# Offering the denominators' products some time behind the modelled landing of p, and starting both chains of them one block of f sooner

## The chip, the cores and the metric

The kernel runs on one core of a Trainium2 chip. Its engines are TensorE (PE in the profile; PEld is its weight load), VectorE (DVE), ScalarE (ACT), GpSimd (POOL) and SyncE (SP). Here POOL and SP mostly issue DMA transfers, each from a queue of its own: q0 is POOL's and q1 is SP's. The metric is the device time of one execution in microseconds, as the median of several runs.

## The reference, cut to what matters

The input x has 2048 tokens of 640 columns. The output is a mix of two branches, weighted by a gate per token:

```
g   = sigmoid(sum(x * gate_w))
# branch a: linear attention, 32 heads of 20
q, k, v = x @ wqkv, split by heads
phi(t)  = (t + 1 if t > 0 else exp(t)) + 1e-6
kv  = sum over tokens of phi(k)^T v ;  z = sum over tokens of phi(k)
num = phi(q) @ kv ;  den = phi(q) . z + 1e-6
a   = (num / den) @ wo
# branch b: gated linear unit, 1536 wide
b   = (sigmoid(x @ w_gate) * (x @ w_up)) @ w_down
out = g * a + (1 - g) * b
```

The change concerns `den`: the sum, over the 20 elements of a head, of phi(q) times z.

## The kernel before, in words

All products are done in three TensorE passes on operands split in a high and a low part (`mm3`, lines 404 to 406). The splitting is work for ScalarE (line 417) and VectorE (line 421), so that both engines are busy with preparing operands and with taking results out of PSUM while TensorE multiplies. Many products use a two by two scheme with sums of operands (steps s1 to s7 of `Block`), which saves products and costs sums.

The tokens are in four groups `g` of 512. First come the keys, kv and z, and M = kv @ wo, which is stored in `m_dram`. Then the groups 2 and 3 (`pr` = 1) and afterwards the groups 0 and 1 (`pr` = 0) go through two phases. `q_phase` makes p = phi(q) and stores it in `p_dram`. `f_phase` runs over 12 blocks `f` of 128 hidden columns of branch b: the steps 3, 4, 5 of block f, step 1 of block f + 1, step 6 of f, step 2 of f + 1 and step 7 of f. From f = 3 on, an odd block also holds the down products of the pair of blocks before it (`down_pair`), so that odd blocks are about twice as long as even ones. At the end M, scaled p and the sums of branch b are put together.

In the phase of `pr` = 0 the weights come back from scratch memory in their split form: `load_form` loads the tiles `wg`, `wu` and `ws` of block f + 2 after steps 2, 6 and 7 of f, and `load_wf` loads, after an odd block, the three pieces of `wf` for the next down products. All these loads are issued by SP. Meanwhile rows of M are loaded by SP into `mr`, split into `mt`, and stored by POOL in `mp_dram` (`queue_m`).

The denominators are made by `queue_dens` (line 1399), in one chain for the groups 2 and 3 and another for 0 and 1. With the heads interleaved over the partitions, phi(q) . z is a sum of five terms, one per slice u of 128 columns: p of that slice times a column of z, added to `fac[:, g]`. So a chain has these links, in this order:

- load p of u = 0 and 1 for both groups into `pden` (POOL's queue);
- for each u and each group, one product on VectorE (line 1412 for u = 0, line 1414 for the others; the profile shows them as L432 and L425), behind which the load of u + 2 is issued;
- behind the last product of a group, the store of `den_dram`;
- `turn_in`: four loads per group that fold the four partial sums of a head side by side (POOL), and a load of the gates `gs` (SP);
- `factor`: the sums, the reciprocal, the product with the gate (VectorE), and the store of `fac_dram` (POOL);
- `turn_out`: four loads per group that spread the factors over `fac` (SP).

The order of instructions is fixed while the program is written, by a planner, the class `Order`. It keeps a modelled clock for TensorE, ScalarE and VectorE, and a model of the two DMA queues (`Ring` and `Rings`, lines 303 to 361) which gives each transfer a modelled landing. Side work waits in lists. `fill` (line 115) is called after each unit of TensorE's work and takes side work as long as it fits: its modelled end must lie no more than a set slack behind TensorE's clock, and the function `ready` that came with it must give a time that has been reached (`_fits`, line 107). The lists are tried in this order: urgent, the streams with due times, items, lazy, chain, spare. Of `chain` only the first entry is looked at, so an entry that isn't ready holds up the rest of the chain, and the `spare` list gets its turn. The denominators are in `chain`; the splits of M are in `spare`. On the chip each engine carries out its instructions in the order so fixed, and real waits are made by semaphores.

For a product `one(g, u)` the time `ready` is the modelled landing of its p, `st["at", g, u]()`. The table `dens` (line 2011) says at the start of which block of f the two chains are put in the list, for the phase of `pr` = 0.

Of the kernel before, what the change touches and what calls it, by code (L numbers as in the profile page):

```python
# [19 lines left out]
TG = 512  # L20
# [9 lines left out]
class Order:  # L30
# [121 lines left out]
    def _stream(self):  # L152
        best = None
        for name, q in self.streams.items():
            if q and (q[0][4] is None or max(self.pe, self.act if q[0][0] else self.vec) >= q[0][4]()):
# [4 lines left out]
                if best is None or d < best[0]:  # L160
                    best = (d, name)
        if best and (best[0] <= self.pe + EARLY or self._fits(self.streams[best[1]][0])):
            return best[1]
# [136 lines left out]
            self.seeded[out.tensor.name] = at  # L300

EARLY = 2.0
class Rings:

    def __init__(self):
# [62 lines left out]
def v_cost(w):  # L368
    return 0.07 + w / 960

@with_exitstack
def gated_mix_kernel(ctx: ExitStack, tc: tile.TileContext, xt, xn, wk, wv, wo, wst_q, wst_f, out_t):
# [6 lines left out]
    order = Order()  # L379
# [39 lines left out]
    def vec2(out, a, b, op, after=""):  # L419
        order.on_vec(width(out), after, 1.0, out, a, b)  # L420
        nc.vector.tensor_tensor(out, a, b, op=op)  # L421

    def vec3(out, a, scalar, b, op0, op1, after=""):
        order.on_vec(width(out), after, 1.0, out, a, b)
        nc.vector.scalar_tensor_tensor(out, a, scalar, b, op0=op0, op1=op1)  # L425

    def vec1(out, a, s0, s1=None, op0=OP.mult, op1=None, after=""):
        order.on_vec(width(out), after, 1.0, out, a)
        if op1 is None:
            nc.vector.tensor_scalar(out, a, s0, None, op0=op0)  # L430
        else:
            nc.vector.tensor_scalar(out, a, s0, s1, op0=op0, op1=op1)  # L432
# [10 lines left out]
    def add(out, a, b, after=""):  # L443
        vec2(out, a, b, OP.add, after)
# [574 lines left out]
    g = GTBatch(0, [0])  # L1019
# [8 lines left out]
    for c in range(1, 4):  # L1028
        ck = chunks[c]
        if c == 1:  # L1030
# [14 lines left out]
            g = GTBatch(c, batches[c])  # L1045
# [97 lines left out]
        if c > 1:  # L1143
            g = GTBatch(c, batches[c])
# [50 lines left out]
    def tt(name, dt=F32, shape=(P, TG)):  # L1195
        return pw.tile(list(shape), dt, name=name, tag="t", bufs=4)
# [202 lines left out]
    def queue_dens(*gs2):  # L1399

        st = {}

        def load(g, u):
            if u < KC:
                st[g, u] = tt("pden")
                gp.dma_start(st[g, u], p_dram[:, u, g])
                st["at", g, u] = lambda: order.when(st[g, u])

        def one(g, u):
            td = fac[:, g]  # L1410
            if u == 0:
                vec1(td, st[g, u], zcol[:, 0:1], zeps[:, 0:1], OP.mult, OP.add)
            else:
                vec3(td, st[g, u], zcol[:, u:u + 1], td, OP.mult, OP.add)
            load(g, u + 2)
            if u == KC - 1:
                gp.dma_start(den_dram[:, g], td)
                st["at", g, u + 1] = lambda: order.when(den_dram[:, g])

        def turn_in(g):  # L1420
            for j in range(4):
                js = slice(j * H, (j + 1) * H)
                gp.dma_start(fac[js, g].rearrange("h (d c) -> h d c", c=P),
                                  den_dram[:, g, j * P:(j + 1) * P].rearrange("(d h) c -> h d c", h=H))
            st[g, "gs"] = tt("gs")[:, :P]
            sp.dma_start(st[g, "gs"], gate_rep[4 * g:4 * g + 4].rearrange("i h c -> (i h) c"))
            st["at", g, KC + 1] = lambda: max(order.when(fac[:, g]), order.when(st[g, "gs"]))

        def factor(g):
            td = fac[:, g]  # L1430
            q = td[:, :P]
            add(td[:, :2 * P], td[:, :2 * P], td[:, 2 * P:])
            add(q, q, td[:, P:2 * P])
            order.on_vec(5 * P, "")
            nc.vector.reciprocal(q, q)
            vec2(q, q, st[g, "gs"], OP.mult)
            gp.dma_start(fac_dram[:, g], q)
            st["at", g, KC + 2] = lambda: order.when(fac_dram[:, g])

        def turn_out(g):  # L1440
            for d in range(4):
                sp.dma_start(fac[d * H:(d + 1) * H, g].rearrange("h (j c) -> h j c", c=P),
                                  fac_dram[:, g].rearrange("(j h) c -> h j c", h=H))
        order.add(0, 0, lambda: [load(g, u) for u in range(2) for g in gs2], chain=True)
        for u in range(KC):
            for g in gs2:
                order.add(0, v_cost(TG), lambda g=g, u=u: one(g, u), None, lambda g=g, u=u: st["at", g, u](), chain=True)
        for n, (v, fn) in enumerate(((0, turn_in), (2.0, factor), (0, turn_out))):
            for g in gs2:
                order.add(0, v, lambda g=g, fn=fn: fn(g), ("fac", g) if n == 2 else None,  # L1450
                          lambda g=g, n=n: st["at", g, KC + n](), chain=True)
# [556 lines left out]
            phi_q(2 * pr + 1, 0, B.c12, "v")  # L2008
        order.slack(False)

    dens = ({3: (2, 3), 7: (0, 1)}, {})

    def f_steps(f):
        down = f % 2 and f > 1
# [8 lines left out]
    def f_phase(pr, q, hooks={}):  # L2023
# [7 lines left out]
        for f, s in [(0, 1), (0, 2)] + [e for f in range(FC) for e in f_steps(f)]:  # L2031
            order.plan[pr, f, s] = at
            at += mm * n_mm[s]
        order.plan[pr, FC + 1, "d0"] = at - EARLY

# [53 lines left out]
        for f in range(FC):  # L2089
# [3 lines left out]
            if f in dens[pr]:  # L2093
                queue_dens(*dens[pr][f])
# [514 lines left out]
```

## Time and profile before

| what | value |
| --- | --- |
| median of 3 runs | 736.67 us |
| lowest and highest run | 735.58 and 737.15 us |
| span of the profiled execution | 733.0 us |
| TensorE busy | 726.8 us, 99% |
| VectorE busy | 561.7 us, 77% |
| ScalarE busy | 355.1 us, 48% |
| loads of pden by POOL | 20, first and last issued at 448.6 and 567.4 us |
| products of the denominators | 20, first and last begun at 481.2 and 575.0 us |
| granted clock of TensorE | 1.000 |

The span reaches from the first to the last instruction in the profile. The profile does not list a device time of the profiled execution itself, so the span is compared with the times of the runs, which are 2.6 to 4.2 us above it. Of a busy engine the sum of busy time says little here; what counts is at which place TensorE pauses, and for whom.

In the profiled execution the phase of `pr` = 0 has its block f = 2 from about 468 to 481 us, f = 3 to 505, f = 4 to 518, f = 5 to 542, f = 6 to 555, f = 7 to 580 and f = 8 to 593.

In the views, a row of the order of time has the start, the duration, the engine, the line and the operation, "out<-in", and in brackets how long the engine stood idle before it and what ended that. A row of a table by stage has the stage, its length, then the busy time and number of instructions of PE, PEld, DVE, ACT and POOL, the granted clock, the share of the DMA engines and their GB/s. A row of waits has the waiting instruction, whom it waited for, the total, the number of times and the longest. A row of DMA issues has the transfer, the queue, the number, the size, and the median time from issue to landing.

### The profile page before, as it was taken

How to read it: one execution, taken by the hardware profiler on the slowest of the kernel's cores; microseconds unless marked ns; L12 is line 12 of the kernel's file. 1: busy time of each engine (PE TensorE's matmuls, PEld its weight loads, DVE VectorE, ACT ScalarE, POOL GpSimd, SP SyncE). 2: the span in 40 equal slices, each digit the busy share in tenths (PEclk: the TensorE clock that was granted, in tenths of full speed). 3: DMA queues.
4: the chain of work that ended last, by engine and by line, in shares of the span. 5: the costliest groups of instructions: out<-in, count | busy, mean ns of one | idle time of the engine just before them, and what ended most of it. 6: DMA issues, size and time to landing. Idle time of an engine off the chain costs nothing.

```text
span 733.0 us, 10118 instructions
## 1 busy us (share of the span) xinstructions
PE 726.8 (99%) x3575; PEld 622.9 (85%) x3575; DVE 561.7 (77%) x987; ACT 355.1 (48%) x661; POOL 113.9 (16%) x197
## 2 busy tenths in 40 slices
PE   9999999999999999999999999999999999999998
PEld 8999999988788888888888888888887888888886
DVE  4978777987677889898989942566766775689976
ACT  5765648357556653535355363354332232332541
POOL 0211111113211211111211212023011231000000
PEclk9999999999999999999999999999999999999999
DMA  8564748697877866557687568878978596759212
GB/s 268 128 192 112 187 114 249 151 352 265 300 270 264 328 241 236 184 218 253 259 326 267 214 230 292 317 231 281 356 266 317 179 322 197 276 209 372 80 67 102
DMA packets 68873, 173.54 MB, mean 237 GB/s; under 512 B 11690, under 2 KB 31418, under 8 KB 65238
## 3 DMA queue, kind: packets, MB, share of 16 engines
q1 hardware_dynamic: 50342, 103.70, 42.7%
q0 software_dynamic: 18336, 69.03, 26.9%
q8 instruction: 28, 0.46, 0.2%
q14 instruction: 23, 0.19, 0.1%
q10 hardware_dynamic: 144, 0.16, 0.1%
HBM read 103.96 MB, written 63.92 MB: 229 GB/s over the span
## 4 chain that ended last, share of the span: by engine, by line
PE 86%; DMA 6%; issue 3%; DVE 2%; ACT 1%; POOL 1%; SPq 0%; POOLq 0%; ACTq 0%; DVEq 0%
PE ch L404 9%; PE ch L405 9%; PE ch L406 9%; PE cc L404 7%; PE cc L405 7%; PE cc L406 7%; PE dd L404 7%; PE dd L405 7%; PE dd L406 7%; PE rot L404 6%; PE rot L405 5%; PE rot L406 5%; DMA wf<-wd 2%; DMA pden<-p_dram 2%; DMA ws<-wf 2%
## 5 line engine op out<-in xcount | busy, mean ns | idle before, releaser
L417 ACT ACTIVATE c<-ch 128x512 f32<-128x512 f32 x52 | 31.1, 598 | 89.0 <-PE ch L406 88.9
L421 DVE TENSOR_TENSOR hf<-c,hf 128x512 fp32r<-128x512 f32 x75 | 51.2, 688 | 20.7 <-ACT hf L417 20.3
L421 DVE TENSOR_TENSOR c<-cc,c 128x512 f32<-128x512 f32 x40 | 27.6, 689 | 42.5 <-PE cc L406 30.4
L417 ACT ACTIVATE hf<-c 128x512 fp32r<-128x512 f32 x75 | 46.1, 625 | 26.1 <-DVE c L421 26.1
L404 PE MATMUL ch<-xth,ws 128*128 128x512 f32 x112 | 43.9, 392 | 0.0
L405 PE MATMUL ch<-xtl,ws 128*128 128x512 f32 x112 | 43.6, 390 | 0.0
L406 PE MATMUL ch<-xth,ws 128*128 128x512 f32 x112 | 43.6, 389 | 0.0
L421 DVE TENSOR_TENSOR tb<-rot,tb 128x512 f32<-128x512 f32 (+1 forms) x61 | 39.4, 676 | 3.0 <-PE rot L406 3.0
L421 DVE TENSOR_TENSOR tb<-dd,tb 128x512 f32<-128x512 f32 x44 | 30.2, 687 | 9.3 <-PE dd L406 9.3
L404 PE MATMUL dd<-xrh,wg 128*128 128x512 f32 x90 | 35.2, 391 | 0.0
L406 PE MATMUL dd<-xrh,wg 128*128 128x512 f32 x90 | 35.0, 389 | 0.0
L405 PE MATMUL dd<-xrl,wg 128*128 128x512 f32 x90 | 35.0, 389 | 0.0
L417 ACT ACTIVATE c<-dd 128x512 f32<-128x512 f32 x22 | 13.1, 597 | 41.4 <-PE dd L406 41.4
L404 PE MATMUL cc<-xbh,ws 128*128 128x512 f32 x84 | 32.7, 389 | 0.0
L406 PE MATMUL cc<-xbh,ws 128*128 128x512 f32 x84 | 32.7, 389 | 0.0
L405 PE MATMUL cc<-xbl,ws 128*128 128x512 f32 x84 | 32.7, 389 | 0.0
L421 DVE TENSOR_TENSOR c<-c,c 128x512 f32<-128x512 f32 x46 | 31.6, 688 | 1.3 <-ACT c L417 0.7
L417 ACT ACTIVATE dd<-ch 128x512 f32<-128x512 f32 x22 | 12.8, 582 | 35.1 <-PE ch L406 35.1
L421 DVE TENSOR_TENSOR wst<-wst 128x256 f32<-128x256 f32 (+2 forms) x69 | 27.4, 413 | 1.5
L404 PE MATMUL rot<-pkh,xnh 128*128 128x320 f32 x90 | 28.0, 311 | 0.2 <-DVE gt L421 0.2
L405 PE MATMUL rot<-pkl,xnh 128*128 128x320 f32 x90 | 27.8, 309 | 0.0
L406 PE MATMUL rot<-pkh,xnl 128*128 128x320 f32 x90 | 27.8, 309 | 0.0
(650 smaller groups left out, 2347.3 us busy)
## 6 DMA issues: line engine op xcount, KB each, us to landing
wf<-ws POOLq DMA_DIRECT2D x12, 1152.0 KB, 7.6
ws<-wf SPq DMA_DIRECT2D x11, 1152.0 KB, 9.2
wst<-wst_f SPq DMA_DIRECT2D x12, 640.0 KB, 5.0
wf<-wg POOLq DMA_DIRECT2D x12, 640.0 KB, 6.4
wd<-wd POOLq DMA_DIRECT2D x12, 640.0 KB, 7.9
wg<-wf SPq DMA_DIRECT2D x12, 640.0 KB, 7.3
wf<-wd SPq DMA_DIRECT2D x10, 640.0 KB, 11.0
xnst<-xn SPq DMA_DIRECT2D x16, 320.0 KB, 4.3
```

The lines of the kernel that those rows point to most:

```text
L404: nc.tensor.matmul(out, l_hi, r_hi, start=first, stop=False, skip_group_check=True)
L405: nc.tensor.matmul(out, l_hi, r_lo, start=False, stop=False, skip_group_check=True)
L406: nc.tensor.matmul(out, l_lo, r_hi, start=False, stop=last, skip_group_check=True)
L417: nc.scalar.activation(out, src, fn, **kw)
L421: nc.vector.tensor_tensor(out, a, b, op=op)
```

## The change

A constant of 5 us is added to the time from which each product of p with z may be taken. And both chains are put in the list one block sooner: that of the groups 2 and 3 at the start of f = 2 in place of f = 3, that of 0 and 1 at f = 6 in place of f = 7. Nothing else of the program text is changed; the order that the planner gives can change from f = 2 of the second phase on.

```
+DEN_LAG = 5.0
+
...
         for u in range(KC):
             for g in gs2:
-                order.add(0, v_cost(TG), lambda g=g, u=u: one(g, u), None, lambda g=g, u=u: st["at", g, u](), chain=True)
+                order.add(0, v_cost(TG), lambda g=g, u=u: one(g, u), None, lambda g=g, u=u: st["at", g, u]() + DEN_LAG, chain=True)
...
-    dens = ({3: (2, 3), 7: (0, 1)}, {})
+    dens = ({2: (2, 3), 6: (0, 1)}, {})
```

## The prediction

> **What bounds the kernel now.** I read the page's first part, then the waits of TensorE (PE) and of its weight loads, then the order of time around each wait.
>
> ```profile
> span 733.0 us, 10118 instructions
> PE 726.8 (99%) x3575; PEld 622.9 (85%) x3575; DVE 561.7 (77%) x987; ACT 355.1 (48%) x661; POOL 113.9 (16%) x197
> ```
>
> TensorE is busy for 99% of the span, so the change, which takes no product from TensorE, can win only what TensorE loses in gaps. From 440 us on, where the change can reach, the views of waits name two that matter:
>
> ```profile
> PE rot L404 <- DVE tb L421: 1.0, 1, 1.0
> PEld dd L404 <- DMA wf<-wd: 0.5, 1, 0.5
> ```
>
> Matmul starts give the loss more exactly than those idle times do:
>
> ```profile
> 517.82 0.39 PE L404 MATMUL ch<-xth,ws 128*128 128x512 f32 x1
> 518.04 0.39 PE L405 MATMUL ch<-xtl,ws 128*128 128x512 f32 x1
> 518.27 0.39 PE L406 MATMUL ch<-xth,ws 128*128 128x512 f32 x1
> 518.74 0.50 PE L404 MATMUL dd<-hf,wf 128*128 128x512 f32 x1
> 519.08 0.40 PE L405 MATMUL dd<-hf,wf 128*128 128x512 f32 x1
> ...
> 566.54 0.50 PE L404 MATMUL cc<-hf,wf 128*128 128x512 f32 x1
> 566.88 0.40 PE L405 MATMUL cc<-hf,wf 128*128 128x512 f32 x1
> 567.12 0.40 PE L406 MATMUL cc<-hf,wf 128*128 128x512 f32 x1
> 568.49 0.47 PE L404 MATMUL rot<-hf,wf 128*128 128x512 f32 x1 [0.97 <-DVE tb L421]
> 568.80 0.39 PE L405 MATMUL rot<-hf,wf 128*128 128x512 f32 x1
> ```
>
> Undisturbed, one product of 512 columns follows the last by (518.27 - 517.82) / 2 = 0.23 us. Around 518 two steps take 0.47 and 0.34, an excess of 0.24 + 0.11 = 0.35 us. Around 567 three steps take 0.34, 1.37 and 0.31, an excess of 0.11 + 1.14 + 0.08 = 1.33 us. Together 1.68 us; I found no other step from 440 to 680 us that exceeds its width's pace by more than 0.06 us. This is the ceiling of the gain.
>
> The stall at 567 waits for VectorE (DVE), and VectorE is late for the reason that the change is about:
>
> ```profile
> 562.74 0.75 DVE L425 SCALAR_TENSOR_TENSOR fac<-pden,zcol,fac 128x512 f32<-128x512 f32 x1 [2.53 <-DMA pden<-p_dram]
> ...
> 567.67 1.28 DVE L421 TENSOR_TENSOR tb<-rot,tb 128x512 f32<-128x512 f32 x2
> ```
>
> A denominator product stood at the head of VectorE for 2.53 us because its p had not landed; the additions behind it move back by as much, and the one that frees the PSUM buffer TensorE wants, tb<-rot, begins only at 567.67. The 0.35 us at 518 is another matter: weights of the down product that landed late.
>
> **The planner and p.** The planner prices a load of p (256 KB on POOL's queue, lines 337 to 361) at 2.2 us of lag, 1.25 x 128 x (7 + 0.0377 x 2048) / 16000 = 0.84 us of transfer and 0.5 us: 3.5 us. The trace has, for the load issued at 555.92 us and for all twenty:
>
> ```profile
> pden<-p_dram POOLq DMA_DIRECT2D x1, 256.0 KB, 6.7
> ...
> DMA to landing us min/median/max: 3.0/5.9/8.9
> ```
>
> So a product can be put up to 5.4 us too early. With 5 us more it is offered 8.5 us behind the modelled issue, which covers all but the extreme of 8.9. The lag adds no instruction.
>
> **The change part by part.** A chain has 10 loads of p, 10 products, 2 stores, 8 loads turning the result in, 2 gate loads, 2 x 5 small VectorE operations, 2 stores and 8 loads turning it out. Their number stays. Each chain's products cost VectorE:
>
> ```profile
> L425 DVE SCALAR_TENSOR_TENSOR fac<-pden,zcol,fac x16: 743/746/753, 483.8 to 575.0; 128x512 f32<-128x512 f32 x16
> L432 DVE TENSOR_SCALAR fac<-pden,zcol,zeps x4: 537/538/542, 481.2 to 555.5; 128x512 f32<-128x512 f32 x4
> ```
>
> 8 x 0.746 + 2 x 0.538 = 7.0 us. Is there room one block sooner? The stages f=2, f=3, f=4, f=6 and the first half of f=7:
>
> ```profile
> 468.00:480.60 12.60, 12.60 (x57) 10.45 (x56) 6.55 (x11) 4.47 (x8) 0.00 (x0) 1.00 0.63 205
> 480.60:505.00 24.40, 24.40 (x109) 20.14 (x108) 16.30 (x25) 13.10 (x23) 9.72 (x18) 1.00 0.77 256
> 505.00:518.00 13.00, 13.00 (x59) 10.78 (x58) 10.81 (x18) 5.58 (x10) 1.16 (x3) 1.00 1.00 346
> 542.00:554.50 12.50, 12.50 (x56) 10.33 (x56) 6.56 (x11) 4.47 (x8) 0.00 (x0) 1.00 1.02 399
> 554.50:567.00 12.50, 12.50 (x56) 10.17 (x55) 9.06 (x15) 4.87 (x9) 2.68 (x5) 1.00 0.79 311
> ```
>
> The third number of busy time is VectorE's. f=2 leaves 12.60 - 6.55 = 6.05 us free, f=6 leaves 5.94. Products of the first pairs there are hidden under TensorE at no cost; uncovered, each would cost its 0.75 us.
>
> *First chain.* Its first loads are ready early, since POOL runs ahead; the rows of POOL's queue for both chains:
>
> ```profile
> 448.57 1.62 POOL L361 DMA_DIRECT2D pden<-p_dram  x3
> ...
> 500.67 4.37 POOL L361 DMA_DIRECT2D fac<-den_dram  x8
> ...
> 538.36 2.15 POOL L361 DMA_DIRECT2D pden<-p_dram  x4
> 555.92 1.06 POOL L361 DMA_DIRECT2D pden<-p_dram  x2 [15.41 <-DVE fac L432]
> ```
>
> Issued from 448.57 on, they are offered, even with the lag, by about 462, before f=2 begins at 468; so the first four products move by a block, to 469 to 472 (estimate). The third and fourth pair follow 8.5 us behind their loads, at 479 to 481, the last at about 490. Before, the last pair ended at 493.77 + 1.41 = 495.2:
>
> ```profile
> 493.77 1.41 DVE L425 SCALAR_TENSOR_TENSOR fac<-pden,zcol,fac 128x512 f32<-128x512 f32 x2
> ```
>
> The chain's results therefore leave some 4 us sooner, not 12: the lag gives two thirds of the block back. Eight turn-in transfers, issued from 500.67 on, move to about 496, out of f=4's stage, where the DMA share is 1.00.
>
> *Second chain.* Its loads stand behind a store on POOL and go out at 538.36 anyway. f=6 begins at 542; with 3.5 to 5 us of modelled flight (four loads in a row share it) and the lag, the first pairs come at 547 to 550, the third at 558, the last at 567 to 569. Two pairs (2.5 us of VectorE) leave f=7, and the 2.53 us stall is gone since each product is offered 8.5 us behind its load. VectorE reaches tb<-rot up to 2.5 us sooner, more than the 1.33 us that TensorE lost. Behind the lag only the chain's own turn-in and factor are held; spare work (the splits of M) goes ahead of it. The factors are first used at 635.9, so a few us there cost nothing:
>
> ```profile
> L425 DVE SCALAR_TENSOR_TENSOR pl<-pl,fac x9: 682/687/689, 635.9 to 665.1; 128x512 f32<-128x512 f32 x9
> ```
>
> *The late weights at 518.* SyncE's queue (SPq) around them, and the landings:
>
> ```profile
> 481.09 20.51 SPq L361 DMA_DIRECT2D mr<-m_dram  x12
> ...
> 505.09 0.32 SPq L361 DMA_DIRECT2D ws<-wf  x1
> 505.45 2.15 SPq L361 DMA_DIRECT2D wf<-wd  x3
> ...
> 524.33 7.70 SPq L361 DMA_DIRECT2D fac<-fac_dram  x8
> ...
> 542.60 2.42 SPq L361 DMA_DIRECT2D wf<-wd  x3
> ```
>
> The first wf piece, issued at 505.45, and the first two of f=6, from 542.60, landed after
>
> ```profile
> wf<-wd SPq DMA_DIRECT2D x1, 640.0 KB, 13.2
> ...
> wf<-wd SPq DMA_DIRECT2D x2, 640.0 KB, 10.4
> ```
>
> So wf landed at 518.65 where it was wanted at 518.50, in a stage whose DMA engines are full and whose first microseconds hold the turn-in. Moving 512 KB of turn-in ahead of it frees 512 KB / 346 GB/s = 1.5 us (estimate), enough for the 0.35 us. Bounds: 0.35 gained, or, if an M load holds SP in front of ws and wf, up to 1.5 lost. I take the gain; 0.15 us of lateness is easily undone.
>
> **Sum.** 1.33 + 0.35 = 1.68 us off the profiled execution: span 733.0 to 731.3. The runs, 735.58 to 737.15, lie 2.6 to 4.2 us above that span; I keep the median's 3.7 us, so 736.67 - 1.68 = 735.0 us.
>
> **Rivals.** (A) *Weights late in f=6, or still late in f=4.* The third and fourth pair's loads, 1 MB, now go out at 549 to 552, into a stage at share 1.02 and 399 GB/s: 2.6 us of transfer. The first wf pieces land at 542.60 + 10.4 = 553.0; the first product that reads them starts at 555.64, a margin of 2.6 us:
>
> ```profile
> 555.64 0.39 PE L404 MATMUL dd<-hf,wf 128*128 128x512 f32 x1
> ```
>
> If all of it goes ahead of wf, nothing is left; with 256 KB more, 0.7 us are lost. If f=4's 0.35 also stays: 736.67 - 1.33 + 0.0 to 0.7 = 735.3 to 736.0. For it: both stages are full; against: half these loads come behind the landing.
>
> The Trainium skill (DMA: Bandwidth & Descriptors, Queues, rings and completion order) says that each DMA engine takes turns packet by packet between the rows it has work for; by that rule POOL's loads would halve SP's flow for as long as they last, which is rival A's bad end and not its mild one. No row here separates it from a plain queue.
>
> (B) *SyncE held in front of the weights: slower.* If the factors come before about 502, turn-out is placed ahead of f=3's last weight loads. Its eight issues held SP for 7.70 us at 524.33; there they would push wf from 505.45 to about 511, the landing to 524, and TensorE would lose about 5.5 us at 518 against 0.35 now: 736.67 - 1.33 + 5.2 = 740.5. It decides at 505: turn-out issued before or after wf<-wd. Against: the factors need the turn-in landed, about 503 to 505, and a store behind them.
>
> (C) *Another wait takes the place.* The splits of M go ahead of held products, and their loads too arrive later than the planner thinks; the longest such wait of VectorE was 2.13 us at 526.44 without a loss on TensorE:
>
> ```profile
> 526.44 0.82 DVE L421 TENSOR_TENSOR mt<-mr,mt 128x640 fp32r<-128x640 f32 x1 [2.13 <-ACT mt L417]
> ```
>
> Placed among the tb additions it would cost about what the p wait did: 736.67 - 1.68 + 1.3 = 736.3.
>
> (D) *The change misses.* VectorE's lateness at 567 could come as much from the ten products and additions crowded there; then the 1.33 stays: 736.67.
>
> **Chances.** Forecast 0.40, A 0.22, B 0.10, C 0.15, D 0.13. About 0.2% (1.5 us) is what a measurement of this kernel can tell from no change. The forecast, 1.68 us, lies barely beyond it, so I count three quarters of it and a third of A as faster: 0.30 + 0.07 = 0.37. Slower is B with a little of C: 0.11. The rest, 0.52, is the same. Range: down to 734.4, since the ceiling of 1.68 leaves only the spread of runs below 735.0; up to 737.0, which takes in A, C and D and leaves B out.
>
> **What would show it.** Right: the first product of each chain one block sooner (about 469 and 548), no fac wait on pden, a steady 0.23 us of TensorE at f=7, wf landed before the down products of f=5. Wrong: a wait of weight loads on wf<-wd over 0.5 us at 518 or 555 (A), fac<-fac_dram ahead of wf<-wd on SP (B), TensorE waiting for tb behind mt (C), or the same gap without a p wait (D).

## Result, and the profile after

| | before | after |
| --- | --- | --- |
| median of 11 runs | 736.61 us | 734.14 us |
| lowest and highest run | 734.43 to 737.75 us | 733.01 to 735.28 us |
| ratio, 95% interval | | 0.9973, 0.9963 to 0.9982 |
| span of the profiled execution | 733.0 us | 731.7 us |
| time of the profiled execution | not listed | 733.42 us |

The changed kernel is faster by 0.27% (0.18 to 0.37%), about 2.0 us. Taken off the 736.67 us of the forecast, that is 734.7 us: within the range on record, near the forecast of 735.0 us and somewhat beyond it. The median of the changed kernel's own runs, 734.14 us, lies 0.3 us below the range. The runs after list span and time together, and the time is 1.7 to 1.8 us longer than the span in each. The profiled execution of before therefore took about 733.0 + 1.7 = 734.7 us (an estimate): some 1.9 us less than its kernel's median.

In the profile of the changed kernel all line numbers below the new constant are two higher (L404 is now L406, L421 is L423, L425 is L427, L432 is L434). The page's first part:

```profile
span 731.7 us, 10116 instructions
PE 726.3 (99%) x3575; PEld 622.4 (85%) x3575; DVE 561.7 (77%) x987; ACT 354.5 (48%) x661; POOL 114.3 (16%) x197
```

The work is the same; the span is 1.3 us shorter. The waits from 440 us on: TensorE itself has none, and of the weight loads only these remain, where before showed 1.0 us behind tb and 0.5 us behind wf:

```profile
PEld rot L406 <- DVE tb L423: 0.2, 1, 0.2
PEld dd L406 <- DMA wf<-wd: 0.2, 1, 0.2
```

The order of time on TensorE at the place of the 1.33 us loss, now in steps of 0.23 us:

```profile
567.01 0.39 PE L408 MATMUL cc<-hf,wf 128*128 128x512 f32 x1
567.24 0.39 PE L406 MATMUL rot<-hf,wf 128*128 128x512 f32 x1
567.47 0.39 PE L407 MATMUL rot<-hf,wf 128*128 128x512 f32 x1
```

And on VectorE, the first chain's products and then part of the second's:

```profile
469.16 0.99 DVE L434 TENSOR_SCALAR fac<-pden,zcol,zeps 128x512 f32<-128x512 f32 x2
...
477.82 2.07 DVE L427 SCALAR_TENSOR_TENSOR fac<-pden,zcol,fac 128x512 f32<-128x512 f32 x3
...
487.84 1.41 DVE L427 SCALAR_TENSOR_TENSOR fac<-pden,zcol,fac 128x512 f32<-128x512 f32 x2
...
493.62 1.40 DVE L427 SCALAR_TENSOR_TENSOR fac<-pden,zcol,fac 128x512 f32<-128x512 f32 x2
...
551.46 0.99 DVE L434 TENSOR_SCALAR fac<-pden,zcol,zeps 128x512 f32<-128x512 f32 x2
552.37 0.74 DVE L427 SCALAR_TENSOR_TENSOR fac<-pden,zcol,fac 128x512 f32<-128x512 f32 x1
...
565.96 1.28 DVE L423 TENSOR_TENSOR tb<-rot,tb 128x512 f32<-128x512 f32 x2
...
574.59 0.75 DVE L427 SCALAR_TENSOR_TENSOR fac<-pden,zcol,fac 128x512 f32<-128x512 f32 x1
```

No product has a wait in brackets any more, and the addition tb<-rot starts at 565.96 in place of 567.67. The first chain starts a block sooner (469.16) but its last pair stands at 493.62, where before had it at 493.77: the whole block was given back.

**A measure for all kernels below.** I add up, from 440 us on, the steps between starts of matmuls as far as they exceed the pace of their width by more than 0.06 us. This sum of TensorE's losses and the span of the profiled executions go together: span minus loss is 730.7 to 731.6 us in all fourteen. The 0.9 us by which these differ lie before 440 us, where the change cannot reach: with the losses summed from the start of the span, span minus loss is 727.8 to 728.1 us. So the losses account for the spans, and each can be looked up at its place.

| kernel (profiled execution) | losses by place, us | sum | span |
| --- | --- | --- | --- |
| before | 518: 0.35; 567: 1.33 | 1.69 | 733.0 |
| before, second execution | 507: 0.37; 518: 1.02; 531: 0.18; 567: 1.34 | 2.93 | 733.7 |
| before, third execution | 496: 0.32; 508: 0.68; 519: 0.54; 531: 0.23; 567: 1.39 | 3.19 | 734.3 |
| after | none over 0.1 | 0.08 | 731.7 |
| after, second execution | 492: 0.16; 518: 0.41; 530: 0.33 | 0.91 | 731.7 |
| second chain only | 508: 0.11; 518: 1.03; 531: 0.25 | 1.40 | 732.5 |
| first chain only | 518: 0.64; 567: 1.33 | 1.98 | 732.7 |
| earlier start only | 492: 0.44; 566: 1.45; 593 to 596: 1.98; 675: 0.84 | 4.74 | 735.8 |
| lag only | 518 to 522: 2.81; 531 to 533: 1.52 | 4.35 | 735.3 |
| no late p, second chain | 492: 2.24; 510: 1.58; 522 to 534: 1.08 | 4.92 | 736.0 |
| no late p, both chains | 518: 0.19 | 0.19 | 731.6 |
| after, and a lag on M | 554 to 558: 1.29 | 1.29 | 732.7 |
| after, first chain at f = 1 | 496: 0.21; 518: 0.39 | 0.61 | 731.5 |
| after, both | 496: 0.60 | 0.69 | 731.4 |

### The profile page after: what moved, and what is told of

It reads as the page before. It is cut to its first block, busy times and chain, and to the rows that moved or that the text cites. A ratio compares the mean times of both kernels' runs of the same rounds, so it can differ in the third digit from the quotient of the medians.

```text
span 731.7 us, 10116 instructions
## 1 busy us (share of the span) xinstructions
PE 726.3 (99%) x3575; PEld 622.4 (85%) x3575; DVE 561.7 (77%) x987; ACT 354.5 (48%) x661; POOL 114.3 (16%) x197
## 4 chain that ended last, share of the span: by engine, by line
PE 93%; ACT 2%; DVE 2%; issue 1%; DMA 1%; POOL 1%; POOLq 0%; ACTq 0%
PE ch L406 10%; PE ch L408 10%; PE ch L407 10%; PE cc L406 8%; PE cc L408 8%; PE cc L407 8%; PE dd L406 7%; PE dd L408 7%; PE dd L407 7%; PE rot L406 6%; PE rot L408 6%; PE rot L407 6%; DMA p_dram<-qe 1%; PE rot L1525 1%; DMA xnh<-wk 0%
## 5 line engine op out<-in xcount | busy, mean ns | idle before, releaser
L423 DVE TENSOR_TENSOR hf<-c,hf 128x512 fp32r<-128x512 f32 x75 | 51.1, 686 | 20.3 <-ACT hf L419 19.8
L423 DVE TENSOR_TENSOR c<-cc,c 128x512 f32<-128x512 f32 x40 | 27.6, 689 | 39.1 <-PE cc L408 27.2
L406 PE MATMUL ch<-xth,ws 128*128 128x512 f32 x112 | 43.8, 391 | 0.0
L423 DVE TENSOR_TENSOR tb<-rot,tb 128x512 f32<-128x512 f32 (+1 forms) x61 | 39.4, 673 | 3.0 <-PE rot L408 3.0
L423 DVE TENSOR_TENSOR tb<-dd,tb 128x512 f32<-128x512 f32 x44 | 30.2, 686 | 11.0 <-PE dd L408 10.9
L406 PE MATMUL dd<-xrh,wg 128*128 128x512 f32 x90 | 35.2, 391 | 0.0
L423 DVE TENSOR_TENSOR c<-c,c 128x512 f32<-128x512 f32 x46 | 31.6, 687 | 2.6 <-ACT c L419 2.0
L406 PE MATMUL cc<-xbh,ws 128*128 128x512 f32 x84 | 32.7, 389 | 0.0
L423 DVE TENSOR_TENSOR wst<-wst 128x256 f32<-128x256 f32 (+2 forms) x69 | 27.4, 412 | 1.5
L406 PE MATMUL rot<-pkh,xnh 128*128 128x320 f32 x90 | 28.1, 312 | 0.1
```

What stands on the lines that cost most here:

```text
L406: nc.tensor.matmul(out, l_hi, r_hi, start=first, stop=False, skip_group_check=True)
```

## Experiments

### The second chain alone, and the first alone

Both keep the lag for one chain only, and start the other where it was.

```
+    dens = ({3: (2, 3), 6: (0, 1)}, {})
+    st["at", g, u]() + (DEN_LAG if gs2[0] == 0 else 0.0)
```

> Only the second chain has the change (f=6, 5 us of lag); the first is as before. Theory 1, the wait for p in the second chain is what cost TensorE its time: the whole gain is kept, 1.3 to 2.5 us (ratio 0.9966 to 0.9982), the steps of TensorE at 566 to 569 are even, no product waits for pden in f=7. Theory 3, the first chain's turn-in made the weights late at 518: part of the gain is missing, 0.35 us or more.

Measured: 735.12 us (734.27 to 736.61, 11 runs) beside 736.68 of before (33 runs), ratio 0.9978 (0.9969 to 0.9987). The loss at 567 is gone.

```
+    dens = ({2: (2, 3), 7: (0, 1)}, {})
+    st["at", g, u]() + (DEN_LAG if gs2[0] == 2 else 0.0)
```

> Only the first chain has the change (f=2, 5 us of lag); the second is as before. Theory 1: no change, within 0.5 us of before; the product that waits 2.5 us for pden at 560 to 563 and TensorE's gap of about 1.3 us behind it are there. Theory 3: 0.35 us or more are gained, and the first wf piece lands clearly before TensorE wants it in f=5.

Measured: 735.22 us (734.11 to 736.58), ratio 0.9979 (0.9971 to 0.9988). The loss at 567 and its p wait are there as before, in the order of time on TensorE:

```profile
566.87 0.40 PE L408 MATMUL cc<-hf,wf 128*128 128x512 f32 x1
568.26 0.47 PE L406 MATMUL rot<-hf,wf 128*128 128x512 f32 x1 [0.99 <-DVE tb L423]
```

VectorE's waits for p in before, and the one that is left here:

```profile
DVE fac L425 <- DMA pden<-p_dram: 4.5, 3, 2.5
...
DVE fac L427 <- DMA pden<-p_dram: 2.5, 1, 2.5
```

So the second chain is worth 736.68 - 735.12 = 1.6 us, about the 1.33 us of the gap. And the first chain, which I had costed at nothing, is worth 736.68 - 735.22 = 1.5 us. The two add up to 3.0 us; the change as a whole measured 736.61 - 734.14 = 2.5 us by medians in the result (2.0 us by the ratio), and 736.64 - 733.48 = 3.2 us in the repetition below. What the first chain's gain consists of the profiled execution of before cannot show, since it lost nothing before 518; that was the new question.

### The earlier start alone, and the lag alone

```
+DEN_LAG = 0.0
+    dens = ({2: (2, 3), 6: (0, 1)}, {})
```

> Both chains one block sooner, lag 0. Theory 1, it is the wait for p: products of the later pairs stand 1 to 3 us at the head of VectorE in f=2 and f=6; where they stand between additions of down products TensorE loses about as much as before, elsewhere nothing: 734.5 to 737.5 us. In the written order one turn-out now stands ahead of a ws load on SyncE. Theory 2, it is the crowding of f=7: the gain of 2.0 us or more is complete without the lag.

Measured: 735.48 us (734.86 to 737.73), ratio 0.9985 (0.9976 to 0.9995). Five p waits, 5.5 us in all, and a gap of the old size at 567, in the order of time on TensorE:

```profile
567.09 0.40 PE L408 MATMUL cc<-hf,wf 128*128 128x512 f32 x1
568.48 0.47 PE L406 MATMUL rot<-hf,wf 128*128 128x512 f32 x1 [0.99 <-DVE tb L423]
```

On SyncE a part of turn-out has come to stand ahead of the weights of the block pair after:

```profile
578.76 1.74 SPq L363 DMA_DIRECT2D fac<-fac_dram  x4
580.62 0.35 SPq L363 DMA_DIRECT2D ws<-wf  x1
581.02 2.96 SPq L363 DMA_DIRECT2D wf<-wd  x3
```

TensorE stood 1.5 us for wf in two waits. So starting sooner alone does not heal the late p, and in this execution it was not free.

This kernel also shows what the lag does to the chain's length. VectorE's products of the first chain, from the second pair on:

```profile
477.41 2.73 DVE L427 SCALAR_TENSOR_TENSOR fac<-pden,zcol,fac 128x512 f32<-128x512 f32 x4
...
487.53 0.75 DVE L427 SCALAR_TENSOR_TENSOR fac<-pden,zcol,fac 128x512 f32<-128x512 f32 x1
490.49 0.75 DVE L427 SCALAR_TENSOR_TENSOR fac<-pden,zcol,fac 128x512 f32<-128x512 f32 x1 [2.21 <-DMA pden<-p_dram]
```

The first pair stands at 468.75, and the second follows only at 477.41, with no lag and with its p landed by 457.19: the planner's order puts no product in between. In the changed kernel the second pair stands at 477.82. So these 8.7 us are not the lag's doing. What the lag does show in is the chain's end: the last two products begin at 487.53 and 490.49 here, at 493.62 and 494.28 in the changed kernel, 4 to 6 us later.

```
+DEN_LAG = 5.0
+    dens = ({3: (2, 3), 7: (0, 1)}, {})
```

> Both chains where they were, lag 5 us. Theory 1: no product waits for pden any more, so the gain of 1.3 to 2.5 us is there, though the products now spread into f=4 and f=8; what may take it back is a factor or turn-out that comes later, up to 1 us. Theory 2, the crowding of f=7: no gain, since all ten products stay in f=7 and f=8.

Measured: 737.38 us (736.87 to 738.29), ratio 1.001 (1.0001 to 1.002): no p wait, no gap at 567, and yet not faster. The held products let splits of M go ahead of them. The two longest of four waits of TensorE that took the gap's place:

```profile
PE dd L406 <- DMA wf<-wd: 1.7, 1, 1.7
PE cc L406 <- DVE tb L423: 0.7, 1, 0.7
```

SyncE's queue ahead of the first of them:

```profile
504.94 1.77 SPq L363 DMA_DIRECT2D mr<-m_dram  x4
506.76 1.10 SPq L363 DMA_DIRECT2D ws<-wf  x1
507.90 3.24 SPq L363 DMA_DIRECT2D wf<-wd  x3
```

VectorE in order of time ahead of the second:

```profile
531.34 0.83 DVE L423 TENSOR_TENSOR mt<-mr,mt 128x640 fp32r<-128x640 f32 x1 [2.61 <-ACT mt L419]
532.08 0.68 DVE L423 TENSOR_TENSOR tb<-cc,tb 128x512 f32<-128x512 f32 x1
```

Rows of M stand on SyncE ahead of the weights, so wf is issued at 507.90 where before had 505.45; and a split of M stands among the additions to tb and makes VectorE stand 2.61 us. The second is what rival C described: a wait of 0.7 us, and with the uneven steps around it 1.5 us of loss from 531 to 533. So the lag pays only together with the earlier start. The earlier start without the lag pays 736.68 - 735.48 = 1.2 us in time, though its profiled execution shows no gain: that one was the slowest of its eleven runs, so its row of losses isn't typical, and where the 1.2 us come from is open.

### p that is never late: crowding or waiting

Here the instructions of VectorE, ScalarE, TensorE and SyncE stay in the order of before, but the loads for the slices u = 2 to 4 are left out: the products read p of slice u - 2 again, so the denominators are other numbers. The planner still prices the loads.

```
+    if g < 2 and u >= 2:
+        st[g, u] = st[g, u - 2]
+        gp.model(st[g, u], p_dram[:, u, g])
```

> The order of before on every engine, but the six loads of p for u = 2, 3 and 4 of the second chain are left out and their products read the p of u - 2: the output is another one, and 1.5 MB less are moved. Theory 1: no wait at 560 to 563, no gap at 567, 1.3 to 2 us faster, as with the second chain's change alone (ratio about 0.998). Theory 2, crowding: the gap at 567 stays, ratio 1.000.

Measured: 734.95 us (734.06 to 737.69, 12 runs) beside 735.85 of before, ratio 0.9991 (0.9981 to 1.0002). That is 0.7 us, at most 1.4, where I had expected 1.3 to 2: by itself no verdict. In the profiled execution, the slowest of the twelve, TensorE loses nothing any more behind 535 us, so the gap of f = 7 is gone. But it loses 4.9 us in f = 3 to f = 5, in the stretch of the first chain, whose p is still loaded here. VectorE in order of time (lines four higher than in before):

```profile
490.52 0.75 DVE L429 SCALAR_TENSOR_TENSOR fac<-pden,zcol,fac 128x512 f32<-128x512 f32 x1 [3.04 <-DMA pden<-p_dram]
492.89 2.14 DVE L429 SCALAR_TENSOR_TENSOR fac<-pden,zcol,fac 128x512 f32<-128x512 f32 x3 [1.62 <-DMA pden<-p_dram]
494.95 0.82 DVE L425 TENSOR_TENSOR mt<-mr,mt 128x640 fp32r<-128x640 f32 x1
```

ScalarE in the same stretch:

```profile
493.44 0.74 ACT L421 ACTIVATE mt<-mr 128x640 fp32r<-128x640 f32 x1 [3.65 <-DMA mr<-m_dram]
...
494.56 1.08 ACT L421 ACTIVATE tb<-rot 128x512 f32<-128x512 f32 x2
```

And TensorE, which waits for ScalarE:

```profile
495.20 0.50 PE L408 MATMUL rot<-hf,wf 128*128 128x512 f32 x1 [1.98 <-ACT tb L421]
```

In these rows ScalarE stands for rows of M (mr) until 493.44 and frees the buffer of rot only behind that; TensorE loses 2.2 us. VectorE stands 4.7 us for p in the same stretch, but it is not what TensorE waits for: the rows of M had been issued at 480.8 to 482.1, before VectorE stood, and landed late by themselves, as p did. The same with both chains (`if u >= 2`), 12 loads fewer:

> The same for both chains: twelve loads left out, 3 MB less, the order of before on every engine. Theory 1, waits for p in both chains cost TensorE: as fast as the whole change, ratio 0.996 to 0.998, and faster than without the second chain's waits alone by 0.5 us or more. Theory 4: no faster than without the second chain's waits alone.

Measured: 733.08 us (732.4 to 733.32, 5 runs), ratio 0.9956 (0.9943 to 0.9969), losses 0.19 us. VectorE at the place of the gap has the crowd of before, all ten products of the second chain in f = 7, from 555.10 to 574.04, of which this stretch shows one:

```profile
563.94 0.74 DVE L429 SCALAR_TENSOR_TENSOR fac<-pden,zcol,fac 128x512 f32<-128x512 f32 x1
565.33 0.69 DVE L425 TENSOR_TENSOR c<-cc,c 128x512 f32<-128x512 f32 x1 [0.64 <-ACT c L421]
565.93 1.28 DVE L425 TENSOR_TENSOR tb<-rot,tb 128x512 f32<-128x512 f32 x2
```

VectorE is early enough to stand 0.64 us for other work ahead of tb<-rot. Crowding (rival D) is not the cause of the gap; the late p is. Leaving out all twelve loads is worth 0.44%, 3.2 us, and the first chain's six, between this kernel and the one above, 734.95 - 733.08 = 1.9 us. The runs do not part what VectorE's standing costs from what the loads of 256 KB cost the other transfers in f = 3, since both go here.

### The two kernels unchanged, once more

> The kernel before, unchanged, to profile another of its executions and to see what two timings of one program differ by. Ratio 1.000, within 0.001. The profiled execution of before had a span of 733.0, and time less span is 1.7 us in every run that lists both; so it was about 1.9 us faster than the median. Theory 1: in a more usual execution the waits for p cost more, in f=3 too (gaps of TensorE at 489 to 497 and at 567, 2.5 us or more together). Theory 4: the difference lies elsewhere, as at the weights at 518, which no change to the chains touches.

Measured: 736.71 us (735.14 to 738.09, 11 runs) beside 735.85 of the 23 others, ratio 1.0005 (0.9995 to 1.0015). So two medians of one program can lie 0.9 us apart, and a difference of medians of that size says little. The profiled execution (735.41 us) and a third one had losses between 492 and 511 that the first did not have.

> The kernel before once more, for a third profiled execution. Theory 1: gaps of TensorE in f=3 or at 567 that follow a product waiting for pden, 2 us or more in all. Theory 4: the gap at 518 is the one that differs between executions.

Measured: 736.08 us. ScalarE in order of time:

```profile
507.18 0.74 ACT L417 ACTIVATE mt<-mr 128x640 fp32r<-128x640 f32 x1 [5.21 <-DMA mr<-m_dram]
507.83 0.58 ACT L417 ACTIVATE c<-dd 128x512 f32<-128x512 f32 x1
```

TensorE, at the product that needs the buffer:

```profile
508.15 0.39 PE L406 MATMUL cc<-xbh,wu 128*128 128x512 f32 x1
508.95 0.50 PE L404 MATMUL ch<-xth,ws 128*128 128x512 f32 x1 [0.41 <-ACT c L417]
```

Again ScalarE stands for mr and reads c late. This execution was a usual one: the median of the 35 runs of before taken side by side here (11, 23 and this one) is 736.05 us. Between 492 and 511 the kernels that load the first chain's p as before lost 0, 0.37, 1.00 (the three of before), 0.11 (second chain only) and 3.82 us (no late p in the second chain). Those with the lag and the start at f = 2 (after twice, first chain only, and the lag on M below) lost 0, 0.16, 0 and 0, and those that start at f = 1 lost 0.21 and 0.60. So the stretch is one where the first chain's place can matter. But the first group's mean of 1.1 us hangs on the 3.82 of a slowest run; without it, it is 0.4 us, not the 1.5 that the first chain gained. How it gains is not shown.

> The changed kernel once more, beside the next three on one chip. Ratio to before 0.996 to 0.998. Theory 1, now with the splits of M as a second victim (a late p in f=3 delays a split of M on VectorE, the next rows of M land later, ScalarE stands for them and reads PSUM late): what is left over lies at ScalarE's waits for mr and at the weights at 518; time less 1.7 us less TensorE's losses after 440 us is 731.1 +- 0.4, as in the ten profiles so far.

Measured: 733.48 us (733.06 to 735.21, 7 runs) beside 736.64, ratio 0.9964 (0.9952 to 0.9976): the change again. But here 0.41 us are lost at 518, as in before. The profiled execution (733.45 us) is a usual one, as the third of before is, so these two may be compared: the losses fall from 3.19 to 0.91 us; 1.39 us of that lie at 567 and 1.00 - 0.16 = 0.84 us between 492 and 511.

### Can more be had: a lag for the rows of M, and a still earlier first chain

ScalarE's waits for mr remain after the change (11.7 us in four waits). So the splits of M got a lag too:

```
-        order.add(a_cost(D), v_cost(D), fn, "m", lambda: order.when(raw), spare=True)
+        order.add(a_cost(D), v_cost(D), fn, "m", lambda: order.when(raw) + 5.0, spare=True)
```

> The changed kernel, and the splits of M are also offered 5 us behind the modelled landing of their rows. If ScalarE's waits for mr (1.3, 3.4 and 5.0 us in the profile of the changed kernel) still cost TensorE in usual executions, they are gone or under 1 us and 0.3 to 1 us more is gained; if not, the time is that of the changed kernel.

Measured: 734.83 us (733.49 to 739.59, 12 runs), ratio 0.998 (0.9966 to 0.9995). The waits for mr shrink from 11.7 to 0.5 us, and TensorE gains nothing from it; a late wf at 555 to 558 costs 1.3 us instead, in the order of time on TensorE:

```profile
558.69 0.47 PE L406 MATMUL dd<-hf,wf 128*128 128x512 f32 x1 [0.60 <-DMA wf<-wd]
```

This is the place that rival A named.

```
-    dens = ({2: (2, 3), 6: (0, 1)}, {})
+    dens = ({1: (2, 3), 6: (0, 1)}, {})
```

> The changed kernel with the first chain at f=1. The turn-in then comes before 495 us. If the turn-in is what makes the weights of f=5 late, as the prediction had it, wf lands 1 us or more before 518.5 and no gap is left there. But in the written order four turn-out loads now stand ahead of f=3's last ws and wf on SyncE: by the prediction's rival B they hold SyncE and wf lands after TensorE wants it, 1 to 5 us lost at 518, 735 to 739 us.

Measured: 733.69 us (733.34 to 734.77, 7 runs), ratio 0.9964 (0.9953 to 0.9975): the changed kernel's time, not the 735 to 739 us expected. Four of the eight turn-out loads now stand ahead of the weights on SyncE, the very thing of rival B, and the landing of wf shows what it cost. SyncE's queue:

```profile
507.05 2.47 SPq L363 DMA_DIRECT2D fac<-fac_dram  x4
509.61 0.38 SPq L363 DMA_DIRECT2D ws<-wf  x1
510.05 2.19 SPq L363 DMA_DIRECT2D wf<-wd  x3
```

The first piece of wf, issued at 510.05, in the DMA issues (the last number is the time to landing):

```profile
wf<-wd SPq DMA_DIRECT2D x1, 640.0 KB, 8.6
```

It lands at 510.05 + 8.6 = 518.65 us. SyncE's queue in the changed kernel:

```profile
505.64 2.17 SPq L363 DMA_DIRECT2D wf<-wd  x3
```

And the first of these pieces there:

```profile
wf<-wd SPq DMA_DIRECT2D x1, 640.0 KB, 13.0
```

505.64 + 13.0 = 518.64 us: the same landing from an issue 4.4 us earlier. Both edits together:

> First chain at f=1 and the splits of M offered 5 us later. In the written order turn-in and turn-out of the first chain are both through before f=3's ws and wf, with two mr loads fewer ahead of them. If turn-in or SyncE held by mr makes the weights late, wf lands before 518 and the time is 732 to 733.5 us, faster than the changed kernel; if the DMA engines are simply full there, as with the change.

Measured: 733.73 us (733.1 to 734.83, 5 runs), ratio 0.9963 (0.9949 to 0.9976). The first piece of wf landed at 508.54 + 8.5 = 517.04 us, ahead of 518 as hoped, and nothing was lost there; but the time was not the expected 732 to 733.5 us. No version beat the changed kernel measurably.

## Why the prediction was right, and where its steps were not

**The late p of the second chain: right.** The gap at 567 was 1.33, 1.34 and 1.39 us in three executions of before, 1.33 where only the first chain was changed, 1.45 where the products were started earlier without a lag, and gone in each kernel in which the second chain's p is not late. Its price by time, 1.6 us with an interval of 1.0 to 2.3 (0.22% of 736.68, 0.13 to 0.31%), contains the predicted 1.33; leaving out its six late loads alone gave 0.7 us, at most 1.4.

**"The chain's results therefore leave some 4 us sooner, not 12": failed.** The results left at the old time, the first store at 494.66 against 494.81 (POOL's queue in the changed kernel):

```profile
494.66 0.55 POOL L363 DMA_DIRECT2D den_dram<-fac  x1 [0.72 <-DVE fac L427]
...
500.53 4.38 POOL L363 DMA_DIRECT2D fac<-den_dram  x8
```

Turn-in is at 500.53, against 500.67 before. I had put the first two pairs at 469 to 472, but only the first came there. The second stands at 477.82, and it stands at 477.41 without any lag: between 470 and 477 us VectorE was idle only twice, for 0.9 us each, and the planner's order puts no product there. From there on the lag adds up: each load is issued behind a product that was itself held, and the fourth and fifth pairs stand at 487.8 and 493.6, the last products 4 to 6 us later than without the lag.

**"Eight turn-in transfers ... move to about 496", worth 0.35 us at 518: failed.** They did not move, and wf landed at 518.64 against 518.65. In the profiled execution after, the loss at 518 is missing because TensorE came there later, at 518.71 against 518.50. The second execution of the changed kernel lost 0.41 us there. This term of the sum was chance: a margin of 0.15 us isn't to be counted on either way.

**"I keep the median's 3.7 us" around the span: failed.** 1.7 to 1.8 us lie around it. The other 1.9 us were losses of the usual execution that the profiled one happened not to have. The median of before implies a loss of about 736.6 - 1.7 - 731.1 = 3.8 us (an estimate). I took 1.68 us for the ceiling of the gain, while it was the ceiling for one lucky execution.

**The first chain costed at nothing: failed, and this is the missing term.** I named the work that hides its products but didn't price its p waits in f = 3, because TensorE lost nothing there in the profile that I had. The time of the first chain alone puts the term at about 1.5 us; whether it is VectorE's waits or the traffic of the loads stays open. The forecast of 1.68 us came close to the 2.0 of the ratio because a term of 0.35 us that isn't there stood in for part of one of 1.5 us that is. The mechanism at 567 was right; that the sum came out so near was luck.

**The second chain's place: a bit off.** Its first pairs come at 551.5, not at 547 to 550, the last product at 574.6, not 567 to 569, for the same two reasons: with the earlier start alone its first pair stands at 542.69 and the second only at 551.29. That lateness cost nothing that shows: no loss lies behind 531 us in either execution of the changed kernel. Nor did the lag cover every load, as I had it: the longest flight of p was 10.4 us here, beyond the 8.5, and made no wait only because its product came late enough, at 555.10 for a landing at 550.56.

**The rivals.** A: the wf pieces of f = 6 took 11.0 us in place of 10.4, without a loss on TensorE. That used up 0.6 us of the 2.6 of margin; that the extra loads of p did it is not shown. By the Trainium skill (DMA: Bandwidth & Descriptors, Queues, rings and completion order) each DMA engine takes turns packet by packet between the queues' rows, which could have taken the whole margin. The three loads of p in f = 6 went out from 552.29 on, 1.3 us before wf landed at 542.62 + 11.0 = 553.6, so they hardly met and the trace doesn't decide the rule. B: not in the changed kernel; in the kernel that starts the first chain at f = 1 half of its condition held (four of the eight turn-out loads ahead of the weights, wf issued at 510.05 where I had said 511), and the loss at 518 was 0.39 us, not 5.5. My price took the flight of wf for fixed. C: not in the changed kernel, seen with the lag alone, where it lost 1.5 us beside my price of 1.3. D: refuted by the kernel with no late p in either chain, which keeps the crowd and loses nothing at 567.

**What stays open.** How much of the first chain's gain is VectorE no longer standing, and how much is that the loads of p go out 6 to 12 us sooner (the last at 482.44 in place of 490.94). It is open too how the late rows of M, which cost TensorE time in some executions, hang together with the first chain: ScalarE's waits for them are much the same before and after (12.1 and 11.7 us), and taking them away gained nothing. The third execution of before, as slow as the median of the 35 runs taken with it, lost 3.19 us; in the runs of before beside the other kernels the median was 736.6 to 736.7, and what the further 0.6 us were is not placed.

## What to carry to other kernels

An instruction that a planner puts at the head of an in-order engine on a hopeful landing time makes all behind it late. Give the modelled landing a margin of the size that the trace shows between model and landing (only 5 us was tried here), and start the chain sooner, since the margin adds up along a chain whose loads wait for its products. Here the margin alone gained nothing, the earlier start alone 1.2 us, and either alone turned the order of other queues (the rows of M, or turn-out, ahead of weights). Before you count on the idle time of an engine in a stage, look where it lies, and whether the planner's order has a place in it. Compare the time of the profiled execution with the median first: where runs scatter by more than the gain sought, take two or three profiles before calling a sum of gaps a ceiling.

## What the runs showed of the hardware

I had not expected that a transfer issued 4.4 us later would land at the same time. In both cases the DMA engines were nearly full until the landing; the table by stage, f = 4, in the kernel with the first chain at f = 1:

```profile
505.00:518.00 13.00, 13.00 (x59) 10.74 (x59) 9.85 (x17) 5.21 (x9) 1.49 (x3) 1.00 0.91 325
```

And in the changed kernel:

```profile
505.00:518.00 13.00, 13.00 (x59) 10.74 (x58) 10.39 (x18) 5.66 (x10) 1.12 (x2) 1.00 1.01 343
```

The flight was 8.6 us in place of 13.0. This does not show that a later issue costs nothing, because the two kernels differ in more than the issue: with the start at f = 1 the eight turn-in loads go out between 489 and 494 us, in the changed kernel from 500.53 on, just ahead of the weights. A second pair has the same issue and another landing. The kernel with the lag on M issues the piece at 505.58 us, within 0.1 us of the changed kernel:

```profile
505.58 2.28 SPq L363 DMA_DIRECT2D wf<-wd  x3
...
wf<-wd SPq DMA_DIRECT2D x1, 640.0 KB, 11.3
```

It lands 1.7 us sooner, at 516.87. And with no late p in the second chain the piece, issued at 507.46, flew 14.8 us and landed at 522.3. So the flight of one load of 640 KB in this stage was 8.5 to 14.8 us in these kernels, and the time of issue alone did not set the landing. What else is under way must then have a part in it, but which transfers count, and for how much, no run here singles out.
